# Feed-forward's first product by Strassen's seven half-sized ones, norms' roots on GpSimd, and a new instruction order

## The chip, the cores and the metric

One core of a Trainium2 chip runs the whole program. Its engines run side by side and wait for one another by semaphores: TensorE (PE, with weight loads shown apart as PEld), VectorE (DVE), ScalarE (ACT), GpSimd (POOL) and SyncE (SP), which issues nearly all DMAs. The metric is the device time of one execution in microseconds (us), the median of several runs.

## The reference

A transformer block on x of 2048 tokens by 512, all in float32: an attention part with 32 heads and a memory over four segments, then a feed-forward with a squared relu. Both have an adaptive norm before them.

```python
h = _layernorm(x) * (1 + ca) + sa
x = x + ga * _A_ref(h, A_wq, A_wk, A_wv, A_wo, A_beta)
h = _layernorm(x) * (1 + cb) + sb
x = x + gb * _B_ref(h, B_w1, B_b1, B_w2, B_b2)

def _B_ref(x, w1, b1, w2, b2):
    h = jnp.einsum("bsd,df->bsf", x, w1) + b1      # 512 -> 1792
    r = jnp.where(h > 0, h, 0)
    return jnp.einsum("bsf,fd->bsd", r * r, w2) + b2
```

## The kernel before

Each float32 operand is split into a rounded high part (fp32r) and the rest, its low part, and a product is three products: high by high, high by low, low by high.

Tokens are worked on in four sections s of 512. Attention runs section by section and makes up the first part of the program; its scores, masks and exponentials keep DVE and ACT busy beside PE. Each section's first norm, `ln1`, takes sums (`ln_stats`), one root for four token tiles at once (`ln_rstd`, L586-L595) and a scaling (`ln_apply`, L598), then transposes on PE. `ln_rstd` is eleven small DVE steps that need each other: epsilon, a first guess by integer arithmetic, three Newton steps. `ln2`, the second norm before the feed-forward, uses the same helpers.

After attention comes the output projection (`wo_tile`, sums bwop), which adds x and leaves the result in X1, one 512-column tile for each of 16 token tiles g, kept on chip. Then the feed-forward: W1 has 14 blocks f of 128 columns, loaded and split into high and low parts once (`load_w1`, tiles wr and W1) and kept; W2 as well (`load_w2`). For each section and block, `ffn1` makes 12 products of 512 columns into one bank (bh, L1357-L1359), ACT applies relu and square (r, rr; L1367, L1371), DVE squares again in full precision and takes the low part (L1374, L1375). `ffn2` multiplies rr with W2, for four token tiles, into four banks bpf (L1385-L1387) that sum over all f.

What stands in which order: every step is an `op` with an engine, a cost, a due time and its needs. A planner (`Plan`) holds buffers as pools with a number of slots (`POOLS`); a step that needs a slot (`get`) comes after the one that gives it back (`put`). The table `ORDER` lists each engine's steps by number and fixes the order; each engine works through its own list strictly. So a step that waits holds up all behind it on its engine. `z` and `e` are due times for the later stages. r had one slot, rr three, wr two.

## Time and profile before

| | us |
|---|---|
| median of 3 runs (785.7 to 787.88) | 787.33 |
| the profiled execution | 789.56 |
| its span, first to last instruction | 787.8 |
| mean granted TensorE clock | 0.992 of full |
| HBM read / written | 29.91 / 7.34 MB |

On the page, a line of a group has the source line, the engine, the operation, output<-inputs, shapes and count, then busy us and mean ns of one, then the idle time before them with what ended it. A busy time of PE counts modelled ends, so only start-to-start times tell its real pace. The chain of waits follows the last instruction back to what released it.

### The profile page before, as it was taken

The page shows a single profiled execution, that of the slowest core. Times are in us where ns is not written, and L with a number is a line of the kernel's source. Part 1 is how long each engine was busy: PE and PEld are TensorE (multiplying, and loading weights), DVE is VectorE, ACT ScalarE, POOL GpSimd, SP SyncE. Part 2 cuts the span into 40 slices and gives each one's busy share as a digit, 9 for nine tenths or more (in the row PEclk, how much of TensorE's full clock was granted, in tenths as well). Part 3 has the DMA queues.
Part 4 walks back from the last instruction along what each step waited for, and adds up shares of the span by engine and source line. Part 5 has one row for each costly group of instructions (what it writes and reads, how often), then busy time and mean ns, then how long its engine had stood idle before and what let it go on. Part 6 is the DMA issues. An engine that isn't in the chain of part 4 may idle for free. (4 is left out here: it accounts for less than half of the span.)

```text
span 787.8 us, 16571 instructions
## 1 busy us (share of the span) xinstructions
PE 770.6 (98%) x6072; PEld 579.4 (74%) x6075; DVE 533.5 (68%) x1493; ACT 429.0 (54%) x908; POOL 221.2 (28%) x334
## 2 busy tenths in 40 slices
...
GB/s 266 173 175 88 190 212 42 96 97 42 124 96 89 90 76 92 78 115 132 142 115 56 68 136 123 103 67 15 0 1 1 0 107 1 0 1 54 0 1 54
DMA packets 51306, 65.33 MB, mean 83 GB/s; under 512 B 7829, under 2 KB 24985, under 8 KB 51226
## 3 DMA queue, kind: packets, MB, share of 16 engines
...
q10 hardware_dynamic: 152, 0.13, 0.1%
HBM read 29.91 MB, written 7.34 MB: 47 GB/s over the span
## 5 line engine op out<-in xcount | busy, mean ns | idle before, releaser
L863 DVE CUSTOM_DVE_ANT_0 ba<-ba,msk 128x512 f32<-128x512 f32 (+2 forms) x384 | 185.7, 543 | 33.0 <-PE ba L858 29.2
L1045 ACT ACTIVATE pt<-bpb 128x512 f32<-128x512 f32 x320 | 170.7, 619 | 23.4 <-PE bpb L1028 22.0
L1374 DVE TENSOR_TENSOR r<-r 128x512 f32<-128x512 f32 x56 | 38.7, 691 | 139.0 <-ACT rr L1371 138.9
L745 PE MATMUL bqk<-HT,WQK 64*128 64x512 f32 x720 | 105.5, 402 | 2.7 <-DVE mx L863 2.6
L1032 POOL TENSOR_SCALAR_AFFINE_SELECT pt<-pt 128x512 f32<-128x512 f32 x128 | 80.3, 646 | 85.8 <-ACT pt L1045 47.0
L1367 ACT ACTIVATE r<-bh,b1c 128x512 f32<-128x512 f32 x56 | 38.5, 688 | 115.1 <-PE bh L1359 62.0
L1385 PE MATMUL bpf<-W,rr 128*128 128x512 f32 x224 | 87.9, 392 | 0.5 <-DVE X1L L1235 0.5
L1386 PE MATMUL bpf<-W,rr 128*128 128x512 f32 x224 | 87.7, 391 | 0.0
L1387 PE MATMUL bpf<-W,rr 128*128 128x512 f32 x224 | 87.6, 391 | 0.0
L1028 PE MATMUL bpb<-ST 64*128 64x256 f32 (+2 forms) x512 | 80.0, 354 | 2.1 <-DMA ST<-mt 0.8
L1087 PE MATMUL bpv<-pt,VT 128*32 128x512 f32 (+3 forms) x1024 | 80.9, 440 | 0.1
L745 PEld LDWEIGHTS bqk<-HT,WQK 64*128 64x128 f32 x720 | 70.8, 187 | 11.5 <-DVE mx L863 3.0
L858 PE MATMUL ba<-ST 63*128 63x256 f32 (+2 forms) x512 | 77.4, 347 | 1.0 <-DVE mx L863 0.4
L858 PEld LDWEIGHTS ba<-ST 63*128 63x128 f32 x512 | 50.9, 187 | 24.9 <-ACT pt L1045 4.3
L1371 ACT ACTIVATE rr<-r 128x512 fp32r<-128x512 f32 x56 | 35.4, 632 | 59.2 <-PE bpf L1387 58.4
L1028 PEld LDWEIGHTS bpb<-ST 64*128 64x128 f32 x512 | 51.3, 186 | 21.1 <-ACT pt L1045 4.4
L863 DVE DVE_READ_ACCUMULATOR2_ANT mx<- 128x1 f32 x384 | 54.2, 141 | 0.0
L825 PE MATMUL bv<-WVO,HT 64*128 64x512 f32 x384 | 53.3, 395 | 0.0
L1087 PEld LDWEIGHTS bpv<-pt,VT 128*32 128x32 f32 x1024 | 27.6, 109 | 33.2 <-issue 27.5
L1385 PEld LDWEIGHTS bpf<-W,rr 128*128 128x128 f32 x224 | 42.1, 188 | 10.2 <-DVE X1L L1235 0.9
L1386 PEld LDWEIGHTS bpf<-W,rr 128*128 128x128 f32 x224 | 42.1, 188 | 9.2
L1387 PEld LDWEIGHTS bpf<-W,rr 128*128 128x128 f32 x224 | 42.0, 188 | 9.2
...
## 6 DMA issues: line engine op xcount, KB each, us to landing
ST<-sg SPq DMA_DIRECT2D x192, 128.0 KB
...
```

What stands on the lines that cost most here:

```text
L745: m = nc.tensor.matmul(bank(("qk", u, w)), W3(w, k, x, cc * P, (cc + 1) * P)[z], HT[z, y, k], start=(ph == 0 and k == 0 and i == 0), stop= ...
L825: m = nc.tensor.matmul(bank(("v", s, t)), HT[z, x, k, t * P:(t + 1) * P], WVO[z, k, y], start=(ph == 0 and k == 0 and i == 0), stop=(ph == ...
L858: nc.tensor.matmul(dst[:, c0:c0 + n], ST[b:b + 63, 0, sl, qt * P:(qt + 1) * P], ST[b:b + 63, 1, sl, :n], start=True, stop=True)
L863: nc.vector.tensor_tensor_reduce(i, i, msk[:, 512 - n:], scale=1.0, scalar=-3e38, op0=ALU.add, op1=ALU.max, accum_out=o)
L1028: nc.tensor.matmul(dst, ST[b:b + 64, 1, sl, kb * P:(kb + 1) * P], ST[b:b + 64, 0, sl, q0:512], start=True, stop=True)
L1032: nc.gpsimd.affine_select(out=ap, in_=ap, pattern=[[0, ap.shape[1]], [1, P]], compare_op=ALU.is_ge, fill=0.0, base=0, channel_multiplier=-1)
L1045: ns = [act(512, lambda j=j: nc.scalar.activation(buf("PPP"[n], pt)[:, i + j], bank(keys[j]), AF.Exp, scale=0.25), pr[slot] + 0.01 + 0.001 ...
L1087: nc.tensor.matmul(bank(o)[32 * hq:32 * hq + 32, q0:q0 + src.shape[1]], v[:, a:a + 32], src, start=start, stop=stop, tile_position=(0, 32 ...
L1374: n = dve(580, lambda: nc.vector.tensor_tensor(TL[r], TL[r], TL[r], op=ALU.mult), pr + 0.01, after=[h], put=[r])
L1385: nc.tensor.matmul(p, rh, FF["W2"][:, f, 0], start=(f == 0), stop=False)
L1386: nc.tensor.matmul(p, rh, FF["W2"][:, f, 1], start=False, stop=False)
L1387: nc.tensor.matmul(p, rl, FF["W2"][:, f, 0], start=False, stop=(f == NF - 1))
```

## The change

It has three parts, which the planner's table ties together.

**Strassen.** A pair q of W1 blocks (256 columns) by 512 tokens, with the 512 inner rows in halves, is a product of 2x2 blocks. Instead of eight half-sized products (24 matmuls of 512 columns with the three-way split) there are seven of six matmuls of 256 columns each, on sums and differences of blocks. The sums of the tokens' side are made by `ln2` (four, `sub`; the array H2 now has seven blocks), those of W1 by `load_w1` (four, L1404). W1 is no longer kept: it is loaded, summed and split anew for every section (tiles w1r and w1d, two slots each). The products go into two banks, bhx and bhy, and are added on DVE into u and r (one slot each), over which relu, square and the copy to rr run on ACT for the whole pair. X1 of sections 0 to 2 no longer stays on chip: it is stored to HBM and loaded again for `ln2` and for the last sum (tiles x1, xh, xf, six slots together).

**Roots.** `ln_rstd` becomes two GpSimd steps, an addition and a power of -0.5.

**Order.** All five lists of `ORDER` are new, made with a cost under which VectorE and GpSimd do not run at once.

The core of the diff:

```diff
 ORDER = {
     "PE": """
-16 43 27 20 37 63 82 81 84 62 72 79 22 29 28 50 40 51 30 67 52 45 34 18 32 65 80 3 85 23 38 56 78 48 59 77 24 21 60 58
+16 67 26 82 79 74 73 31 37 75 53 27 40 28 78 35 39 50 63 81 17 29 76 54 33 68 65 85 51 83 24 45 3 58 47 77 61 25 32 19
...
+    mhalf = const.tile([P, 4], F32)
+    MHN = op("POOL", 0.1, lambda: nc.gpsimd.memset(mhalf, -0.5), -5.0)
     def ln_rstd(mvs, n):
-        v = small.tile([P, n], F32, name="lnv")
-        y = small.tile([P, n], F32, name="lny")
-        t = small.tile([P, n], F32, name="lnt")
         var = mvs[:, :, 1]
-        nc.vector.tensor_scalar(v, var, EPS_LN, None, op0=ALU.add)
-        nc.vector.tensor_scalar(y.bitcast(I32), v.bitcast(I32), -0.5, float(0x5F3759DF), op0=ALU.mult, op1=ALU.add)
-        for it in range(3):
-            nc.vector.scalar_tensor_tensor(t, y, -0.5, y, op0=ALU.mult, op1=ALU.mult)
-            nc.vector.tensor_tensor(t, t, v, op=ALU.mult)
-            nc.vector.scalar_tensor_tensor(var if it == 2 else y, t, 1.5, y, op0=ALU.add, op1=ALU.mult)
+        nc.gpsimd.tensor_scalar(var, var, EPS_LN, None, op0=ALU.add)
+        nc.gpsimd.tensor_tensor(var, var, mhalf[:, :n], op=ALU.pow)
...
-        r = op("DVE", 2.16, lambda: ln_rstd(TL[mv], 4), p_stat + 0.05, after=st)
+        r = op("POOL", 0.5, lambda: ln_rstd(TL[mv], 4), p_stat + 0.05, after=[*st, MHN])
...
+        keep = [] if last or s == 0 else [("x1", g)]
+        X1N[g] = op("DVE", 0.8, lambda: ln_stats(x1(g), st_all[:, g]), pr + 0.06, after=[n], put=keep)
+        if not last:
+            X1D[g] = sp(lambda: nc.sync.dma_start(x1_dram[s][(g % 4) * P:(g % 4 + 1) * P, :], x1(g)), pr + 0.055, 1 << 18, lat=1.3,
+                        after=[n], put=keep)
...
+        def split(n, i, j, b):
+            v = lambda: tl(i, j).rearrange("p (k n) -> p k n", k=2)
+            h = act(512, lambda: nc.scalar.copy(h2(s, b)[:, 0], v()), pr[2] + 0.02, sbuf=True, after=[*n, *wait])
+            lo = op("DVE", 0.6, lambda: nc.vector.tensor_tensor(h2(s, b)[:, 1], v(), h2(s, b)[:, 0].bitcast(F32), op=ALU.subtract),
+                    pr[2] + 0.03, after=[h], put=[kk(i, j)] if b > 2 else ())
+            H2N[s][b] = [h, lo]
+            return [lo]
+        def sub(o, a, b, after):
+            return op("DVE", 0.6, lambda: nc.vector.tensor_tensor(tl(*o), tl(*a), tl(*b), op=ALU.subtract), pr[2] + 0.025, after=after,
+                      put=[kk(*a), kk(*b)])
...
+            if i == 0:
+                l00 = split(F[0][0], 0, 0, 0)
+                l10 = split(F[0][1], 0, 1, 1)
+        l11 = split(F[1][1], 1, 1, 2)
+        t1 = sub((0, 0), (1, 0), (0, 0), l00 + F[1][0])
+        t3 = sub((1, 0), (1, 1), (1, 0), [t1] + F[1][1])
+        t2 = sub((1, 1), (1, 1), (0, 0), [t1, t3] + l11)
+        t4 = sub((0, 1), (0, 1), (1, 1), [t2] + l10)
+        split([t1], 0, 0, 3)
+        split([t2], 1, 1, 4)
+        split([t3], 1, 0, 5)
+        split([t4], 0, 1, 6)
...
-    def load_w1(f, pr):
-        k = ("wr1", f)
-        wv_ = lambda: wraw(k).rearrange("p (k n) -> p k n", k=KD)
-        n = sp(lambda: nc.sync.dma_start(wv_(), w1[:, f * P:(f + 1) * P].rearrange("(k p) n -> p k n", p=P)), pr - 0.2,
-               1 << 18, after=[N_FFN], get=[("wr", k)])
-        n = act(512, lambda: nc.scalar.copy(FF["W1"][:, f, 0], wv_()), pr, sbuf=True, after=[n], put=[k])
-        W1N[f] = dve(512, lambda: nc.vector.tensor_tensor(FF["W1"][:, f, 1], wv_(), FF["W1"][:, f, 0].bitcast(F32), op=ALU.subtract),
-                     pr + 0.01, after=[n], put=[k])
+    def load_w1(s, q, pr):
+        kr, kd = ("w1r", s, q), ("w1d", s, q)
+        def load():
+            TL[kr] = FF["sb"].tile([P, 4, 2, P], F32, name="w1r", tag=f"w1r{PL.slot[kr]}")
+            for h in (0, 1):
+                f = 2 * q + h
+                nc.sync.dma_start(TL[kr][:, 2 * h:2 * h + 2].rearrange("p a k n -> p (a k) n"),
+                                  w1[:, f * P:(f + 1) * P].rearrange("(k p) n -> p k n", p=P))
+        def hi(a, b, o):
+            if kd not in TL:
+                TL[kd] = FF["sb"].tile([P, 2, 7, 2, P], F32R, name="w1d", tag=f"w1d{PL.slot[kd]}")
+            nc.scalar.copy(TL[kd][:, 0, o:o + b - a], TL[kr][:, a:b])
+        def lo(a, b, o):
+            nc.vector.tensor_tensor(TL[kd][:, 1, o:o + b - a], TL[kr][:, a:b], TL[kd][:, 0, o:o + b - a].bitcast(F32), op=ALU.subtract)
+        def sums():
+            r = TL[kr]
+            for o, a, b, f in ((1, 0, 1, ALU.add), (0, 2, 0, ALU.subtract), (2, 1, 2, ALU.subtract), (3, 3, 2, ALU.subtract)):
+                nc.vector.tensor_tensor(r[:, o], r[:, a], r[:, b], op=f)
+        n = sp(load, pr - 0.2, 1 << 19, 2, after=[N_FFN], get=[("w1r", kr)])
+        h = act(768, lambda: hi(1, 4, 0), pr, sbuf=True, after=[n], get=[("w1d", kd)])
+        l = dve(768, lambda: lo(1, 4, 0), pr + 0.01, after=[h])
+        n = op("DVE", 1.36, sums, pr + 0.02, after=[l])
+        h2_ = act(1024, lambda: hi(0, 4, 3), pr + 0.03, sbuf=True, after=[n])
+        l2_ = dve(1024, lambda: lo(0, 4, 3), pr + 0.04, after=[h2_], put=[kr])
+        W1N[s, q] = ([h, l], [h2_, l2_])
...
-    def ffn1(s, f, pr):
-        i = s * NF + f
-        b, r, rr = ("h", s, f), ("r", s, f), ("rr", s, f)
-        def mm(k):
-            h2 = LT["H2"][s % 2]
-            p = bank(b)
-            wh, wl = FF["W1"][:, f, 0, k], FF["W1"][:, f, 1, k]
-            nc.tensor.matmul(p, wh, h2[:, 0, k], start=(k == 0), stop=False)
-            nc.tensor.matmul(p, wh, h2[:, 1, k], start=False, stop=False)
-            nc.tensor.matmul(p, wl, h2[:, 0, k], start=False, stop=(k == KD - 1))
-        n = None
-        for k in range(KD):
-            n = pe("F", 0.699, lambda k=k: mm(k), pr + 0.001 * k, after=[n] if k else [W1N[f], *H2N[s]], get=() if k else [("#D", b)])
-        F1[s, f] = n
-        def relu():
-            TL[r] = FF["sb"].tile([P, 512], F32, name="r", tag=f"r{PL.slot[r]}")
-            nc.scalar.activation(TL[r], bank(b), AF.Relu, bias=b1c[:, f:f + 1])
-        def square():
-            TL[rr] = FF["sb"].tile([P, 2, 512], F32R, name="rr", tag=f"rr{PL.slot[rr]}")
-            nc.scalar.activation(TL[rr][:, 0], TL[r], AF.Square)
-        n = act(512, relu, pr + 0.01, sc=1, after=[n, n_b1], get=[("r", r)], put=[b])
-        h = act(512, square, pr + 0.011, sbuf=True, after=[n], get=[("rr", rr)])
-        n = dve(580, lambda: nc.vector.tensor_tensor(TL[r], TL[r], TL[r], op=ALU.mult), pr + 0.01, after=[h], put=[r])
-        n = dve(512, lambda: nc.vector.tensor_tensor(TL[rr][:, 1], TL[r], TL[rr][:, 0].bitcast(F32), op=ALU.subtract), pr + 0.012,
-                after=[n, h], put=[r])
-        return n
+    def ffn1(s, q, pr):
+        x, y, kd = ("hx", s, q), ("hy", s, q), ("w1d", s, q)
+        r, rr, u = ("r", s, q), ("rr", s, q), ("u", s, q)
+        wa, wb = W1N[s, q]
+        B = H2N[s]
+        def mm(a, b, key, c):
+            w, m, p = TL[kd], h2(s, b), bank(key)[:, 256 * c:256 * c + 256]
+            for k in (0, 1):
+                nc.tensor.matmul(p, w[:, 0, a, k], m[:, 0, k], start=k == 0, stop=False)
+                nc.tensor.matmul(p, w[:, 0, a, k], m[:, 1, k], start=False, stop=False)
+                nc.tensor.matmul(p, w[:, 1, a, k], m[:, 0, k], start=False, stop=k == 1)
+        def prod(i, key, c, pr, after, **kw):
+            a, b = {1: (1, 0), 2: (2, 1), 3: (6, 2), 4: (0, 6), 5: (4, 3), 6: (5, 4), 7: (3, 5)}[i]
+            return pe("F", 0.712, lambda: mm(a, b, key, c), pr + 0.001 * i, after=[*(wa if a < 3 else wb), *B[b], *after], **kw)
+        rt = lambda: TL[r]
+        two = lambda t: t.rearrange("p (c n) -> p c n", c=2)
+        def u1():
+            TL[u] = FF["sb"].tile([P, 2, 256], F32, name="u", tag=f"u{PL.slot[u]}")
+            nc.scalar.copy(TL[u][:, 0], bank(x)[:, :256])
+        def u34():
+            TL[r] = FF["sb"].tile([P, 4, 256], F32, name="r", tag=f"r{PL.slot[r]}")
+            nc.vector.tensor_tensor(rt()[:, 0:4:3], two(bank(y)), TL[u][:, 1:2, :].to_broadcast([P, 2, 256]), op=ALU.add)
+        def add(o, a, b):
+            return lambda: nc.vector.tensor_tensor(o(), a(), b(), op=ALU.add)
+        p1 = prod(1, x, 0, pr, [], get=[("#D", x)])
+        n1 = act(256, u1, pr + 0.001, after=[p1], get=[("u", u)])
+        p6 = prod(6, x, 1, pr + 0.01, [p1])
+        n2 = dve(256, add(lambda: TL[u][:, 1], lambda: TL[u][:, 0], lambda: bank(x)[:, 256:]), pr + 0.011, after=[p6, n1])
+        p7 = prod(7, y, 0, pr + 0.02, [p6], get=[("#D", y)])
+        p5 = prod(5, y, 1, pr + 0.03, [p7])
+        n3 = dve(512, u34, pr + 0.031, after=[p5, n2], get=[("r", r)])
+        n4 = dve(256, add(lambda: rt()[:, 1], lambda: rt()[:, 0], lambda: bank(y)[:, 256:]), pr + 0.032, after=[n3])
+        p2 = prod(2, x, 0, pr + 0.04, [p5, n1, n2])
+        n5 = dve(256, add(lambda: rt()[:, 2], lambda: TL[u][:, 0], lambda: bank(x)[:, :256]), pr + 0.041, after=[p2, n3], put=[x, u])
+        p4 = prod(4, y, 0, pr + 0.05, [p2, n4])
+        p3 = prod(3, y, 1, pr + 0.06, [p4], put=[kd])
+        F1[s, q] = p3
+        n6 = dve(512, add(lambda: rt()[:, 0:4:3], lambda: rt()[:, 0:4:3], lambda: two(bank(y))), pr + 0.061, after=[p3, n4], put=[y])
+        def relu(i):
+            nc.scalar.activation(rt()[:, 2 * i:2 * i + 2], rt()[:, 2 * i:2 * i + 2], AF.Relu, bias=b1c[:, 2 * q + i:2 * q + i + 1])
+        a = [act(512, lambda i=i: relu(i), pr + 0.062 + 0.001 * i, sbuf=True, sc=1, after=[n6, n4, n5, n_b1]) for i in (0, 1)]
+        def high():
+            TL[rr] = FF["sb"].tile([P, 2, 4, 256], F32R, name="rr", tag=f"rr{PL.slot[rr]}")
+            nc.scalar.copy(TL[rr][:, 0], rt())
+        n = act(1024, lambda: nc.scalar.activation(rt(), rt(), AF.Square), pr + 0.064, sbuf=True, after=a)
+        h = act(1024, high, pr + 0.065, sbuf=True, after=[n], get=[("rr", rr)])
+        n = dve(1024, lambda: nc.vector.tensor_tensor(TL[rr][:, 1], rt(), TL[rr][:, 0].bitcast(F32), op=ALU.subtract), pr + 0.066,
+                after=[h], put=[r])
+        return [h, n]
...
+        if f == NF - 3:
+            n = X1L2[g]
+            if s < NS - 1:
+                n = sp(lambda: nc.sync.dma_start(xt_(), x1_dram[s][t * P:(t + 1) * P, :]), pr - 0.5, 1 << 18, after=[X1D[g], N_FFN], get=[("x1", xf)])
+            F2[s, t, "x"] = dve(512, lambda: nc.vector.tensor_tensor(xt_(), xt_(), gab, op=ALU.add), pr, after=[n_b2, n])
...
-        for f in range(NF):
-            RR[s, f] = ffn1(s, f, z + ST2 * (s * NF + f))
+            ln2(s, [z + ST2 * ((s - 1) * NF + 4 + 2 * t) for t in range(4)], [F1[s - 2, q] for q in range(NF // 2)] if s > 1 else WOL)
+        for q in range(NF // 2):
+            if s:
+                load_w1(s, q, z + ST2 * (s * NF + 2 * q - 3))
+            RR[s, q] = ffn1(s, q, z + ST2 * (s * NF + 2 * q))
```

Three places in the order. First, the root of section 2's first norm, in attention. On DVE before, sg is a query or key tile, lnv, lny and lnt are the root's small tiles, mv the norm's sums:

```order
L784 TENSOR_TENSOR sg<-bqk,sg 128x512
L590 TENSOR_SCALAR lnv<-mv 128x4
L591 TENSOR_SCALAR lny<-lnv 128x4
L593 SCALAR_TENSOR_TENSOR lnt<-lny 128x4
L594 TENSOR_TENSOR lnt<-lnt,lnv 128x4
L595 SCALAR_TENSOR_TENSOR lny<-lnt,lny 128x4
```

Six more steps like the last three follow. Now it stands on GpSimd, between attention's masks (pt) and a marker of one element (hinge):

```order
L806 TENSOR_TENSOR phi0_1870<-phi0_1870,e_1873 128x512
L1044 AFFINE_SELECT pt_1791<-pt_1791 128x4x128
L603 TENSOR_SCALAR mv_1689<-mv_1689 128x4
L604 TENSOR_TENSOR mv_1689<-mv_1689,mhalf_117 128x4
L516 MEMSET hinge_s_116 1x1
```

Eleven steps left DVE, and two joined GpSimd's queue behind its larger ones.

Second, DVE where the feed-forward begins. Before, oT is the output projection's low part, wr a raw block and W1 its split:

```order
L1228 TENSOR_TENSOR oT_7704<-bwot_7690,oT_7704 128x512
L1326 TENSOR_TENSOR W1_7678<-wr_7686,W1_7678 128x512
L1326 TENSOR_TENSOR W1_7678<-wr_7688,W1_7678 128x512
L1326 TENSOR_TENSOR W1_7678<-wr_7728,W1_7678 128x512
L1228 TENSOR_TENSOR oT_7756<-bwot_7747,oT_7756 128x512
L1326 TENSOR_TENSOR W1_7678<-wr_7735,W1_7678 128x512
```

Now, with the first pair's raw w1r_7653 and split w1d_7690:

```order
L1399 TENSOR_TENSOR w1d_7690<-w1r_7653,w1d_7690 128x768
L1404 TENSOR_TENSOR w1r_7653<-w1r_7653 128x256 x4
L1416 TENSOR_TENSOR wr_7669<-wr_7669,gbb_7652 128x512
L1416 TENSOR_TENSOR wr_7671<-wr_7671,gbb_7652 128x512
L1257 TENSOR_TENSOR X1L_70<-bwop_7686,xw_7676 128x512
L1399 TENSOR_TENSOR w1d_7690<-w1r_7653,w1d_7690 128x1024
```

The split of one pair is now three kinds of step, the last of which stands behind W2's scaling and a sum of the projection; the second pair's begins before the first pair's sums u and r.

Third, DVE in the middle of the feed-forward, section 2. Before:

```order
L1374 TENSOR_TENSOR r_9001<-r_9001 128x512
L621 TENSOR_SCALAR xh_8611<-blnq_8963,modc_78 128x256
L1395 TENSOR_TENSOR X11_6245<-bpf_8599,X11_6245 128x512
L1375 TENSOR_TENSOR rr_9005<-r_9001,rr_9005 128x512
L1374 TENSOR_TENSOR r_9050<-r_9050 128x512
```

Now:

```order
L1399 TENSOR_TENSOR w1d_9807<-w1r_9682,w1d_9807 128x768
L1404 TENSOR_TENSOR w1r_9682<-w1r_9682 128x256 x4
L1463 TENSOR_TENSOR u_9822<-u_9822,bhx_9757 128x256
L1489 TENSOR_TENSOR rr_9847<-r_9765,rr_9847 128x1024
L1460 TENSOR_TENSOR r_9864<-bhy_9825,u_9822 128x2x256
L1463 TENSOR_TENSOR r_9864<-r_9864,bhy_9825 128x256
L1510 TENSOR_TENSOR X1L_70<-X1L_70,gab_82 128x512
L1463 TENSOR_TENSOR r_9864<-u_9822,bhx_9757 128x256
```

Where two steps for each block stood, DVE now has W1's split for a later pair (L1399, L1404), the pair's own sums (L1463, L1460) and the low part of the pair before (L1489), which must be done before the next sum may write the single r.

More of the change, by code (lines that the diff above doesn't have):

```diff
@@ L393, in block_kernel @@
     dram = ctx.enter_context(tc.tile_pool(name="dram", bufs=1, space=bass.MemoryType.DRAM))
+    x1_dram = [dram.tile([L, D], F32, name=f"x1_dram{s}") for s in range(NS - 1)]
     o_dram = dram.tile([S, D], F32, name="o_dram")
```

372 lines of the change are left out of this document (204 added, 168 removed), and 12 rows, old and new, of the table ORDER.

## The prediction

> **What bounds the kernel now.** I read the page's busy times and chain of waits first, then the windows, then single rows.
>
> ```profile
> PE 770.6 (98%) x6072; PEld 579.4 (74%) x6075; DVE 533.5 (68%) x1493; ACT 429.0 (54%) x908; POOL 221.2 (28%) x334
> PE 36%; DMA 3%; DVE 2%; issue 1%; ACT 1%; POOL 0%; SPq 0%; POOLq 0%; DVEq 0%; ACTq 0%
> PE bpf L1386 6%; PE bpf L1387 6%; PE bpf L1385 6%; PE bh L1357 6%; PE bh L1358 6%; PE bh L1359 6%; DMA wr<-in_B_w 3%; PE blnq L607 1%; ACT pt L1045 0%; DVE W L1334 0%; DVE W L1326 0%; DVE wr L1332 0%; DVE r L1374 0%; POOL pt L1032 0%; DVE rr L1375 0%
> ```
>
> The chain's six named lines are all the feed-forward: there TensorE (PE) sets the end. The windows (columns: stretch, its length, then busy us and count of PE, PEld, DVE, ACT, POOL, granted clock, DMA share, GB/s) show two regimes.
>
> ```profile
> 150.00:200.00 50.00, 48.91 (x619) 33.96 (x617) 45.36 (x157) 41.95 (x98) 32.52 (x49) 1.00 0.30 72
> 400.00:440.00 40.00, 39.97 (x340) 27.49 (x336) 38.00 (x113) 25.15 (x53) 8.55 (x16) 1.00 0.24 73
> 459.00:540.00 81.00, 79.41 (x354) 64.09 (x354) 62.84 (x132) 34.62 (x60) 0.00 (x0) 1.00 0.35 101
> 540.00:620.00 80.00, 80.00 (x355) 65.00 (x355) 31.48 (x50) 22.04 (x36) 0.00 (x0) 1.00 0.00 1
> ```
>
> Attention (to about 455 us) has VectorE (DVE) at 45 of 50 us and 38 of 40. From 459 us PE is full and DVE is far from it. Whether "full" is true of modelled ends is settled by start-to-start times:
>
> ```profile
> 560.10 0.39 PE L1357 MATMUL bh<-WVO,W 128*128 128x512 f32 x1
> ...
> 574.98 0.40 PE L1386 MATMUL bpf<-W,rr 128*128 128x512 f32 x1
> 29.02 0.28 PE L737 MATMUL bqk<-HT,WQK 128*128 128x256 f32 x1
> ...
> 32.24 0.28 PE L737 MATMUL bqk<-HT,WQK 128*128 128x256 f32 x1
> 544.41 0.60 PE L607 MATMUL blnq<-ident,xh 128*128 128x128 f32 x4
> 544.76 0.48 PE L1357 MATMUL bh<-WVO,W 128*128 128x512 f32 x1
> ```
>
> Between the first two stand 64 steps: 14.88/64 = 0.2325 us for a 512-column product. Between the next two, 27 steps: 3.22/27 = 0.1193 us for a 256-column one of the same type with its own weight load. A transpose takes 0.35/4 = 0.0875. From the first bh (459.29) to the end of the last bpf (783.97) are 324.7 us; 1344 products of the feed-forward and 33 of the output projection at 0.2325, and 52 transposes, make 324.7. PE has no idle time there at all, so a product less is time less, as long as its suppliers keep up.
>
> **The change part by part.**
>
> *Products.* For two blocks of W1 (a pair) before issues 24 products of 512 columns, 24 x 0.2325 = 5.58 us; after issues 7 x 6 = 42 of 256, 42 x 0.1193 = 5.01. There are 4 x 7 = 28 pairs: 28 x 0.57 = **15.9 us less**. The second product stays at 5.58 a pair, so a pair now has 10.6 us of PE.
>
> A rule that speaks against it: the Trainium skill, Perfetto Trace Analysis, Identifying the Most-Contended Engine, says headroom on TensorE is to be judged by the weight loads' busy share, not by matmul busy time. The rows to weigh it by:
>
> ```profile
> 26.90 0.19 PEld L736 LDWEIGHTS bqk<-HT,WQK 128*128 128x128 f32 x1
> 27.02 0.19 PEld L737 LDWEIGHTS bqk<-HT,WQK 128*128 128x128 f32 x1
> ```
>
> Loads of 0.19 start every 0.12, so they overlap each other, and the 256-column products kept their 0.119. By the rule 66 loads a pair at 0.19 would take 12.5 us, more than the 10.6 that the products need; the rows speak for the 10.6.
>
> *VectorE in the feed-forward.* Its price by start-to-start times:
>
> ```profile
> 502.17 0.69 DVE L1375 TENSOR_TENSOR rr<-r,rr 128x512 fp32r<-128x512 f32 x1
> 502.77 0.69 DVE L1326 TENSOR_TENSOR W<-wr,W 128x512 fp32r<-128x512 f32 x1
> 439.45 0.42 DVE L965 TENSOR_TENSOR am<-bmr,den 128x256 f32<-128x256 f32 x1
> 439.79 0.25 DVE L1149 RECIPROCAL dn<-bfin 128x16 f32<-128x16 f32 x1
> 471.86 0.68 DVE L1374 TENSOR_TENSOR r<-r 128x512 f32<-128x512 f32 x1
> 472.58 0.69 DVE L1375 TENSOR_TENSOR rr<-r,rr 128x512 fp32r<-128x512 f32 x1
> ```
>
> 512 columns hold DVE for 0.60, 256 for 0.34, and a step that needs the one just before it starts 0.72 after it, 0.12 late. So 768 columns come to 0.87 and 1024 to 1.14, estimated on the same slope; a dependent 256 is 0.46. Per pair, evacuation was 4 x 0.60 = 2.4; it becomes 3 x 0.34 + 2 x 0.60 + 1.14 + 2 x 0.12 = 3.6. W1's split was 1.2 and done once; it becomes 0.87 + 4 x 0.46 + 1.14 = 3.85 in every section. In section 0 that is 7 x (1.2 + 2.65) = 27 us more, later 7 x 5.05 = 35. Each second norm takes seven more 512 steps (four sums, three splits: 4.2) and loses its root (2.2, below): 2 more. By the windows above, 459:540 would hold 62.8 + 29 = 92 us of DVE against 81 - 4 = 77 of PE: 15 too much. 540:620 would hold 31.5 + 37 = 68 against 76. Some of the surplus moves later, so I counted both engines along the changed order at these prices, from the first split on DVE and the first product on PE: DVE is about 10 us ahead in work from the third pair to the seventeenth (101 against 90 at the ninth, 152 against 141 at the fourteenth), and PE overtakes it only at the twenty-fifth. DVE may begin up to 5 us before PE's first product, so packed without a gap it holds PE back by 5; each of its waits for ACT, PE or a load in those 150 us adds to that. Bounds 0 (the surplus deferred to where PE has more) and 15; I take **+11**, nearer to the upper, since an engine that waits on three others is not packed without gaps. ACT rises to about 5.6 us a pair (a copy of 256, two relus, two passes of 1024, W1's 1.7) and stays hidden behind PE's 10.6; without that cover it would join the chain below.
>
> *A longer chain on one buffer.* r has one slot. Before, a block's chain was relu, square, product, low part; each fits between PE's other work:
>
> ```profile
> L1367 ACT ACTIVATE r<-bh,b1c 128x512 f32<-128x512 f32 x56 | 38.5, 688 | 115.1 <-PE bh L1359 62.0 <-DVE rr L1375 52.9
> L1371 ACT ACTIVATE rr<-r 128x512 fp32r<-128x512 f32 x56 | 35.4, 632 | 59.2 <-PE bpf L1387 58.4
> 442.56 4.05 ACT L1045 ACTIVATE pt<-bpb 128x512 f32<-128x512 f32 x8
> ```
>
> (Eight at 4.05: 0.51 apart.) After, from the fourth product of a pair to that of the next: two products 1.6, sum 0.69, two relus 1.3, square and copy of 1024 columns 1.1 each, low part 1.2, the next pair's first two sums 0.69 + 0.42: about 8.1 us. Behind the waiting sum on DVE's queue stand the next W1 splits, and PE's own queue is in order, so its later products wait too. The chain fits into 10.6, but the changed order puts only 7.7 to 11.2 us of PE work (median 9.2) between the third product of a pair and the fourth of the next; that part of the chain is 6.5 without anything queued in front, and one 1024-column step in front of a link costs 1.1. Bounds 0 and 0.5 x 28 = 14; where DVE sets the pace its stalls are counted already, so I take **+3**, nearer to the chain that fits.
>
> *Roots on GpSimd.* One root on DVE is eleven dependent steps:
>
> ```profile
> 473.19 0.17 DVE L590 TENSOR_SCALAR lnv<-st_all 128x4 f32<-128x4 f32 x1
> ...
> 475.17 0.17 DVE L595 SCALAR_TENSOR_TENSOR st_all<-lnt,lny 128x4 f32<-128x4 f32 x1
> L593 DVE SCALAR_TENSOR_TENSOR lnt<-lny 128x4 f32<-128x4 f32 x24 | 7.0, 294 | 0.8
> 193.99 1.22 POOL L1032 TENSOR_SCALAR_AFFINE_SELECT pt<-pt 128x512 f32<-128x512 f32 x2 [0.29 <-ACT pt L1045]
> 194.01 0.64 DVE L1151 TENSOR_TENSOR dn<-dn,omg 128x16 f32<-128x16 f32 x1
> 195.18 1.28 POOL L629 TENSOR_TENSOR HT<-xt,HT 128x512 fp32r<-128x512 f32 x1
> 195.31 1.19 DVE L1151 TENSOR_TENSOR dn<-dn,omg 128x16 f32<-128x16 f32 x1
> L1006 POOL TENSOR_TENSOR MB<-MB,tm 32x34 f32<-32x34 f32 x32 | 7.8, 245 | 1.4
> L793 POOL TENSOR_SCALAR e<-e 128x512 f32<-128x512 f32 x24 | 35.7, 1486 | 9.7 <-ACT e L789 9.6
> ```
>
> Alone it takes 2.15 us (473.19 to 475.34). The two L1151 rows, of 16 columns, end where GpSimd's instruction ends: VectorE steps with two SBUF inputs wait for GpSimd. That is why L593 means 294 ns, not 160. Five roots lie in attention (four first norms, section 0's second): 5 x 2.15 = 10.8 us of DVE, and the blocked time with it, perhaps 3. The power is in no row: two steps of four columns cost between 2 x 0.25 and 2 x 1.49 us; even 3.0 replaces 2.15 in the norm's own delay, and the norm stands well ahead of its use. POOL is 28% busy, so its queue has room; ahead of a root may stand 1.5 us. Nothing here excludes a loss.
>
> *The order.* Avoiding the blocked pairs can return up to the excess of L1151, L598 and the roots, some 10 us of DVE. Attention's DVE relief is thus 11 to 24 us at 85 to 95% use, and only part of it ends on PE. Bounds -18 and +4 (a new order that fits worse); I take **-7**.
>
> *Transition.* Section 0's seven extra 512 steps (4.2) fall into 400:440, where DVE has 38 of 40, and x1 now goes through 12 stores, on SP's queue past the W1 loads, and 20 loads. **+2** (0 to 5). W1 is read four times: 42 more loads of 256 KB. They lie beside an idle DMA (share 0.00 in 540:620); if that cover fails, a load that lands late stops a pair, for some microseconds each.
>
> **Sum**: -15.9 + 11 + 3 - 7 + 2 = -6.9. The profiled execution took 789.56 us (span 787.8), so 782.7; the median of the three runs is 2.2 lower: **780.5**. A measurement of this kernel can tell about 0.3% (2.4 us) from no change.
>
> **The rivals.**
> 1. *The surplus is deferred*: DVE's extra work finds room behind PE after all, and its relief in attention pays 10. -15.9 + 3 + 3 - 10 + 2 = -18: 769.5. For it: only 31 of 80 us of DVE are busy in 540:620. Against: 92 us of it in 77.
> 2. *Attention gains nothing*: PE, not DVE, ends the waits there, or the new order only shifts them. -15.9 + 11 + 3 + 0 + 2 = 0: 787.5, no change. For it: PE is 49 of 50 busy in 150:200, though by modelled ends.
> 3. *Slower: the pair's chain sets the pace.* Without its term the sum is -9.9, so from 0.35 us of stall a pair (28 x 0.35) the change loses. With a 1024-column step in front at one link in most pairs, 0.8 us: 28 x 0.8 = 22, -9.9 + 22 = +12: 799.5. For it: one slot of r, two queues in order. Against: median 9.2 us of PE work in the place of 6.5.
> 4. *The products do not shrink*: weight loads bind at 0.19, 12.5 us a pair against 11.2 before: 28 x 1.3 = +36, with -7 + 2 near 818. The 0.119 rows speak against it. It is the time that the rule of Perfetto Trace Analysis in the Trainium skill would suggest.
>
> **How the numbers follow.** Forecast (774 to 787): 0.44. Rival 1 (758 to 774): 0.22. Rival 2 (785 to 790): 0.13. Rival 3 (790 to 808): 0.18. Rival 4: 0.03. Faster (below 785): 0.22 and most of the forecast's 0.44: 0.60; within 0.3%: the rest of it and two thirds of rival 2: 0.13; slower: 0.27. The range 762 to 801 leaves out about 0.15 of these. Both signs hold much of the chance, so the forecast's own range, 774 to 787, stands beside it.
>
> **What would show it.** bhx and bhy products at 0.12 start to start confirm the first term. In the windows from 455 us: PE gaps ended by DVE w1d or r in the first 90 us are the second term (VectorE), PE gaps ended by DVE r in all four sections the chain's. The attention terms together (-7 + 2) need the first product against a block of W1 at about 454 us, and 459.29 or later would refute it. The forecast is wrong if the feed-forward's stage (324.7 before) is not 315 to 330 us long, or if its start moves by over 15.

## The result, and the profile after

| | before | after |
|---|---|---|
| first timing, 4 runs each | 786.83 us (785.7 to 787.88) | 778.83 us (774.6 to 781.16) |
| ratio, 95% interval | | 0.9893 [0.9847, 0.9938] |
| second timing, 11 and 5 runs | 787.35 us | 776.87 us |
| ratio, 95% interval | | 0.9857 [0.9836, 0.9879] |
| profiled execution, span | 789.56, 787.8 us | 778.38, 776.7 us |
| first product against W1 | 459.29 us | 460.46 us |
| from it to the last bpf's end (the stage) | 324.7 us | 312.6 us |

The kernel is 8 to 10.5 us faster; 780.5 was predicted. The profiled execution is 11.2 us shorter: the feed-forward's stage 12.1 less, its start 1.2 later. So the total came near while its parts did not: the stage was to be 315 to 330 us long and took 312.6, and its start was to be near 454 us.

The page after (busy times, then the chain of waits):

```profile
PE 756.3 (97%) x6576; PEld 594.2 (77%) x6579; DVE 643.3 (83%) x1643; ACT 509.2 (66%) x990; POOL 233.6 (30%) x351
PE 69%; DVE 16%; ACT 6%; issue 3%; SPq 3%; DMA 2%; POOL 1%; ACTq 0%; DVEq 0%; POOLq 0%
```

VectorE went from 68 to 83% busy. Its 16% of the chain can't be set against the 2% of before: that chain reaches back only to 440 us, this one to the program's start. Between the first product against W1 and the last bpf's end, VectorE is 78.6 of the 312.6 us of this chain. The same windows as before (busy us of PE, PEld, DVE, ACT, POOL, then granted clock, DMA share, GB/s):

```profile
150.00:200.00 50.00, 49.45 (x613) 33.25 (x609) 42.74 (x154) 42.02 (x97) 32.34 (x48) 0.97 0.23 61
400.00:440.00 40.00, 39.68 (x322) 26.40 (x321) 35.34 (x91) 27.59 (x59) 11.15 (x18) 1.00 0.41 123
459.00:540.00 81.00, 79.96 (x503) 70.45 (x502) 79.05 (x137) 51.00 (x74) 0.00 (x0) 1.00 0.39 114
540.00:620.00 80.00, 79.54 (x502) 70.90 (x501) 75.33 (x130) 49.02 (x67) 0.00 (x0) 1.00 0.34 103
```

Attention lost 2.6 us of VectorE in each of the first two stretches. In 459:540 PE and DVE both read as full. By this view alone neither can be called the bound; the runs below had to tell. Single rows of the changed kernel (start, length, engine, line) give the product's price and the stage's start:

```profile
460.46 0.37 PE L1443 MATMUL bhx<-H2a,w1d 128*128 128x256 f32 x1
460.67 0.28 PE L1444 MATMUL bhx<-H2a,w1d 128*128 128x256 f32 x1
460.79 0.28 PE L1445 MATMUL bhx<-H2a,w1d 128*128 128x256 f32 x1
460.90 0.28 PE L1443 MATMUL bhx<-H2a,w1d 128*128 128x256 f32 x1
461.02 0.28 PE L1444 MATMUL bhx<-H2a,w1d 128*128 128x256 f32 x1
461.13 0.28 PE L1445 MATMUL bhx<-H2a,w1d 128*128 128x256 f32 x1
```

From the second to the sixth are 0.46/4 = 0.115 us each: 0.12, as forecast, with a weight load for each. (Over the whole stage of w1_one_sum below, the 1176 products take 140.9 us from start to next start, 0.120 each.) PEld is busy 70.9 of 80 us and binds nothing: in the run w1_one_sum below, where TensorE never waits in the feed-forward, it is busier still (windows, columns as above):

```profile
460.00:540.00 80.00, 79.98 (x514) 72.22 (x513) 71.87 (x118) 53.11 (x77) 0.00 (x0) 1.00 0.42 126
```

### The profile page after: what moved, and what is told of

It reads as the page before. It is cut to its first block, busy times and chain, and to the rows that moved or that the text cites. A ratio compares the mean times of both kernels' runs of the same rounds, so it can differ in the third digit from the quotient of the medians.

```text
span 776.7 us, 17899 instructions
## 1 busy us (share of the span) xinstructions
PE 756.3 (97%) x6576; PEld 594.2 (77%) x6579; DVE 643.3 (83%) x1643; ACT 509.2 (66%) x990; POOL 233.6 (30%) x351
## 4 chain that ended last, share of the span: by engine, by line
PE 69%; DVE 16%; ACT 6%; issue 3%; SPq 3%; DMA 2%; POOL 1%; ACTq 0%; DVEq 0%; POOLq 0%
PE bqk L757 9%; PE bpv L1099 6%; PE bpf L1502 5%; PE bpf L1504 5%; PE bpf L1503 5%; PE ba L870 5%; PE bpb L1040 5%; PE bv L837 4%; PE bhy L1443 3%; PE bhy L1444 2%; PE bhy L1445 2%; ACT pt L1057 2%; SPq L812 2%; PE bwarm L546 2%; DVE w1r L1404 2%
## 5 line engine op out<-in xcount | busy, mean ns | idle before, releaser
L875 DVE CUSTOM_DVE_ANT_0 ba<-ba,msk 128x128 f32<-128x128 f32 (+2 forms) x384 | 186.0, 542 | 33.9 <-PE ba L870 27.1
L1057 ACT ACTIVATE pt<-bpb 128x512 f32<-128x512 f32 x320 | 173.3, 616 | 31.2 <-PE bpb L1040 27.6
L1396 ACT CAST w1d<-w1r 128x768 fp32r<-128x768 f32 (+1 forms) x56 | 52.7, 944 | 76.5 <-PE bhy L1445 58.2
L757 PE MATMUL bqk<-HT,WQK 64*128 64x512 f32 x720 | 101.6, 396 | 0.0
L870 PE MATMUL ba<-ST 63*128 63x256 f32 (+2 forms) x512 | 75.1, 346 | 1.0 <-issue 0.4
L870 PEld LDWEIGHTS ba<-ST 63*128 63x128 f32 x512 | 48.8, 187 | 19.4 <-issue 4.2
L1399 DVE TENSOR_TENSOR w1d<-w1r,w1d 128x768 fp32r<-128x768 f32 (+1 forms) x56 | 60.6, 1085 | 3.2 <-ACT w1d L1396 2.8
L1404 DVE TENSOR_TENSOR w1r<-w1r 128x256 f32<-128x256 f32 x112 | 47.5, 424 | 3.2
L1481 ACT ACTIVATE r<-r,b1c 128x512 f32<-128x512 f32 x56 | 38.4, 719 | 17.8 <-DVE r L1463 17.5
L1504 PEld LDWEIGHTS bpf<-W,rr 128*128 128x128 f32 x224 | 42.0, 188 | 10.0 <-DVE rr L1489 0.3
```

The lines of the kernel that those rows point to most:

```text
L757: m = nc.tensor.matmul(bank(("qk", u, w)), W3(w, k, x, cc * P, (cc + 1) * P)[z], HT[z, y, k], start=(ph == 0 and k == 0 and i == 0), stop= ...
L870: nc.tensor.matmul(dst[:, c0:c0 + n], ST[b:b + 63, 0, sl, qt * P:(qt + 1) * P], ST[b:b + 63, 1, sl, :n], start=True, stop=True)
L875: nc.vector.tensor_tensor_reduce(i, i, msk[:, 512 - n:], scale=1.0, scalar=-3e38, op0=ALU.add, op1=ALU.max, accum_out=o)
L1057: ns = [act(512, lambda j=j: nc.scalar.activation(buf("PPP"[n], pt)[:, i + j], bank(keys[j]), AF.Exp, scale=0.25), pr[slot] + 0.01 + 0.001 ...
L1404: nc.vector.tensor_tensor(r[:, o], r[:, a], r[:, b], op=f)
L1504: nc.tensor.matmul(p, rl, FF["W2"][:, f, 0], start=False, stop=(f == NF - 1))
```

## The experiments

All were timed against the kernel before on the same chip. "After" in the comparisons is the second timing, 0.9857. At 787.5 us, 0.001 of ratio is 0.8 us.

**Attention: the order and the roots.** Two kernels exchange attention between before and after, as far as the instruction lists can be joined; a third moves the roots alone. A fourth has the old order, but all roots on GpSimd, with the new feed-forward.

attn_old_ffn_new: the lists of ORDER up to about 390 us in before's sequence, and

```diff
-        r = op("POOL", 0.5, lambda: ln_rstd(TL[mv], 4), p_stat + 0.05, after=[*st, MHN])
+        r = op("DVE", 2.16, lambda: ln_newton(TL[mv], 4), p_stat + 0.05, after=st)
```

> The changed kernel with the old order of the attention's instructions on every engine up to about 390 us of the plan, and with the first norms' roots back on VectorE; from there on, and in the whole feed-forward, it is the changed kernel. Theory N (the new order and the roots on GpSimd bought nothing that reached the feed-forward): as the changed kernel, 776 to 781 us, ratio to the kernel before 0.986 to 0.992, first product against W1 at 459 to 462 us. Theory P (the prediction's: they bought 5 to 7 us, lost again where attention hands over to the feed-forward): 783 to 787 us, first product against W1 5 us later than in the changed kernel (460.46).

Measured: 780.88 us, 0.9896 [0.9875, 0.9917].

attn_new_ffn_old: the kernel before with after's lists up to about 410 us and, for the first norms,

```diff
-        r = op("DVE", 2.16, lambda: ln_rstd(TL[mv], 4), p_stat + 0.05, after=st)
+        r = op("POOL", 0.5, lambda: ln_power(TL[mv], 4), p_stat + 0.05, after=[*st, MHN])
```

> The kernel before with the changed kernel's order of the attention's instructions up to about 410 us of the plan and the first norms' roots on GpSimd; the end of attention, the hand-over and the feed-forward are those of before. Theory N: 786 to 790 us (the place where the two orders are joined may cost 0 to 4 us), first product against W1 at 458 to 463 us. Theory P: 780 to 783 us, that product at 453 to 455 us.

Measured: 786.73 us, 0.9980 [0.9961, 0.9999].

roots_only: the same line, before's lists.

> The kernel before, old order everywhere, only the four first norms' roots moved from VectorE to GpSimd. Theory N: 786 to 789 us (8.6 us of VectorE less, none of it ends on TensorE). Theory P: half or more of the 8.6 us arrives, 781 to 784 us. A third: the power of 1.05 us and the step of 0.23 to 0.45 us before it stand in front of other GpSimd work and the old order does not fit them: 788 to 792 us.

Measured: 784.51 us, 0.9956 [0.9936, 0.9976].

old_order_roots_ffn_new: attn_old_ffn_new without its diff line, the roots at their old places in the order.

> The changed kernel with the old order of attention up to about 390 us of the plan and all roots on GpSimd. The roots alone, in the kernel before, were worth 3.5 us (ratio 0.9956); the new order with the roots 1.6 us (0.998). Theory R (the roots pay, the new order gives half of it back): 1.5 to 3 us faster than the changed kernel, 3 to 4 us faster than the same with the roots on VectorE (0.9896), ratio 0.985 to 0.987. Rival (what attention gains is lost again at the hand-over, where the new feed-forward waits for something else): as the changed kernel within 1 us.

Measured: 777.01 us, 0.9858 [0.9835, 0.9881].

The roots alone are worth 3.5 us in the old kernel (interval 1.9 to 5.0); theory N falls there, and theory P's half of 8.6 us, 4.3, is inside the interval. In the new one they are worth about 3 (0.9896 to 0.9858; these two intervals overlap by a little). The new order adds nothing in the new kernel (0.9858 to 0.9857, each known to about 2 us); joined to the old feed-forward it stands 1.9 us behind the roots alone, but these intervals overlap too, and the joint may cost that. Theory R's second half falls: the new kernel is no faster with the old order, so the new order gave nothing back there, and it gained nothing that can be measured. The root's price on GpSimd, grouped by form (busy us, mean ns):

```profile
L604 POOL TENSOR_TENSOR mv<-mv,mhalf 128x4 f32<-128x4 f32 x4 | 4.2, 1046 | 0.3
L603 POOL TENSOR_SCALAR mv<-mv 128x4 f32<-128x4 f32 x4 | 0.9, 228 | 3.0 <-DVE mv L596 2.9
```

1.27 us together, inside the bounds of 0.5 and 3.0.

**VectorE in the feed-forward.** First the changed kernel once more, beside the next runs:

> The changed kernel itself, timed beside the next three on one chip: ratio to the kernel before 0.985 to 0.992, 777 to 781 us at this chip's level of the kernel before.

Measured: 776.87 us, 0.9857 [0.9836, 0.9879]; stage 312.6.

w1_one_sum takes VectorE work away; three of four sums are left out, so the products are of other numbers:

```diff
-            for o, a, b, f in ((1, 0, 1, ALU.add), (0, 2, 0, ALU.subtract), (2, 1, 2, ALU.subtract), (3, 3, 2, ALU.subtract)):
+            for o, a, b, f in ((1, 0, 1, ALU.add),):
```

> The changed kernel with one of the four sums on W1's quarters for each pair; the other three are left out, so VectorE has 3 x 0.46 = 1.4 us less in each of 28 pairs and TensorE the same work. Theory D (VectorE, packed without a gap, sets the pace for the first ten or so pairs, and holds TensorE back by 5.7 us in all): 4 to 5.5 us faster than the changed kernel, 773 to 775 us, ratio 0.981 to 0.985, the gain all there by the eleventh pair. Rival E (TensorE sets the pace, VectorE's work is hidden): 777 to 780 us. The prediction's size (11 us from VectorE): 767 to 769 us.

Measured: 771.17 us, 0.9778 [0.9754, 0.9802]: 6.2 us under after, more than theory D's 4 to 5.5 and less than the prediction's 11. The stage itself is 308.2 us, 4.4 less, as D has it, and TensorE alone is 307.0 us of its chain of waits. Of the other 1.8 us the two profiles show 0.4 ahead of the stage (458.96 against 459.39); what is left is inside the intervals.

w1_low_twice adds VectorE work:

```diff
-        l = dve(768, lambda: lo(1, 4, 0), pr + 0.01, after=[h])
+        l = dve(768, lambda: (lo(1, 4, 0), lo(1, 4, 0)), pr + 0.01, after=[h])
```

> The changed kernel with the first low part of W1 (768 columns, 0.95 us) computed twice for each pair: 28 x 0.9 = 25 us more on VectorE, nothing else. Theory D (VectorE paces the first half of the feed-forward, TensorE overtakes it late): by the count of both engines' work VectorE is then ahead until the twenty-fourth pair, by up to 18.6 us instead of 5.7, so 11 to 14 us more than the changed kernel, with the feed-forward's stage at 324 to 327 us (312.6). Rival E (TensorE paces): 0 to 4 us more.

Measured: 793.59 us, 1.0078 [1.0060, 1.0097]; stage 330.3. That is 17.4 us more for 28 x 0.96 = 27 us of work: theory D's direction, but more than its 11 to 14, and the stage is over its 324 to 327. The second pass also stands in front of the links of r's chain, and TensorE waits 6.8 us for r there (1.1 in after_again); that this is the surplus was not tested.

Where the time goes shows in VectorE's L1460, the sum that each pair makes once after its fourth product (p5). The first product against W1, then the ninth and the twenty-eighth L1460, of after_again:

```profile
459.39 0.37 PE L1443 MATMUL bhx<-H2a,w1d 128*128 128x256 f32 x1
554.67 0.69 DVE L1460 TENSOR_TENSOR r<-bhy,u 128x512 f32<-128x512 f32 x1
756.42 0.69 DVE L1460 TENSOR_TENSOR r<-bhy,u 128x512 f32<-128x512 f32 x1
```

and of w1_one_sum:

```profile
458.96 0.37 PE L1443 MATMUL bhx<-H2a,w1d 128*128 128x256 f32 x1
550.26 0.69 DVE L1460 TENSOR_TENSOR r<-bhy,u 128x512 f32<-128x512 f32 x1
751.58 0.69 DVE L1460 TENSOR_TENSOR r<-bhy,u 128x512 f32<-128x512 f32 x1
```

After its first product, after_again needs 95.28 us to the ninth pair and w1_one_sum 91.30: 4.0 behind. At the last pair it is 297.03 against 292.62: 4.4. The same difference, pair by pair, for the runs with this feed-forward on which this part and the next ones rest (us behind w1_one_sum, each worked out from such rows and counted from its own first product):

| pair | 1 | 3 | 5 | 7 | 9 | 10 | 13 | 17 | 21 | 28 |
|---|---|---|---|---|---|---|---|---|---|---|
| after_again | 0.3 | 0.9 | 2.2 | 3.1 | 4.0 | 3.8 | 3.8 | 4.6 | 5.3 | 4.4 |
| trans_full | 0.4 | 1.0 | 2.3 | 3.2 | 4.0 | 3.9 | 3.9 | 4.7 | 5.3 | 4.4 |
| trans_order | 4.5 | 5.0 | 6.3 | 7.3 | 8.1 | 8.0 | 8.0 | 8.8 | 9.5 | 8.6 |
| half_square | 0.3 | 0.9 | 2.2 | 3.1 | 4.0 | 3.8 | 3.4 | 4.1 | 4.8 | 3.7 |
| gate_late_trans | 0.3 | 0.3 | -0.1 | -0.2 | 0.1 | 2.9 | 2.9 | 6.6 | 7.3 | 7.6 |
| w1_low_twice | 1.1 | 3.6 | 6.5 | 9.5 | 12.3 | 13.1 | 15.0 | 19.4 | 21.9 | 22.1 |
| chain_longer | 0.4 | 2.3 | 4.4 | 6.5 | 8.6 | 9.5 | 11.5 | 15.8 | 19.6 | 23.4 |

The changed kernel's loss is made in pairs 1 to 9 and stays. The prediction's count had 101 us of VectorE's work to the ninth L1460. In the first profile after, the rows of VectorE's first split of W1 and of that sum are:

```profile
456.26 0.96 DVE L1399 TENSOR_TENSOR w1d<-w1r,w1d 128x768 fp32r<-128x768 f32 x1 [0.52 <-ACT w1d L1396]
555.71 0.69 DVE L1460 TENSOR_TENSOR r<-bhy,u 128x512 f32<-128x512 f32 x1
```

From the start of the one to the end of the other are 100.1 us, and VectorE is idle in only 2.4 of them, in pieces of at most 0.33: it is packed. In w1_one_sum the same stretch is 95.5 us long, with 9.5 idle.

**The chain on r.** chain_longer doubles one step of it on ScalarE, and leaves VectorE's work alone:

```diff
             nc.scalar.copy(TL[rr][:, 0], rt())
+            nc.scalar.copy(TL[rr][:, 0], rt())
```

> The changed kernel with the copy of r to its high part (1024 columns, about 1.05 us on ScalarE) done twice for each pair: r's chain is 1.05 us longer in each of 28 pairs, VectorE and TensorE have the same work. Theory S (the chain has room: with three sums left out the stage came to 308.2 us, which is TensorE's work alone, so the chain's term is nothing): 0 to 2 us more than the changed kernel. Rival C (the chain is at its limit where VectorE isn't): from 10 us up to 28 x 1.05 = 29 us more, with TensorE's gaps ended by r in all four sections.

Measured: 795.42 us, 1.0094 [1.0068, 1.0119]; stage 331.2, so 18.6 us more for 28 x 1.05 = 29. Theory S falls. In its windows (columns as above) TensorE loses 2 to 3.6 us each, in 580:620 too, where it is busy for all 40.00 us in the changed kernel:

```profile
460.00:540.00 80.00, 76.45 (x475) 66.42 (x474) 74.90 (x130) 54.11 (x76) 0.00 (x0) 1.00 0.36 112
540.00:580.00 40.00, 37.93 (x233) 32.97 (x233) 36.25 (x62) 27.01 (x36) 0.00 (x0) 1.00 0.44 139
580.00:620.00 40.00, 37.61 (x238) 32.83 (x237) 34.55 (x60) 24.39 (x35) 0.00 (x0) 1.00 0.16 47
```

and among its waits (waited for: us in total, times, longest) r's are by far TensorE's largest:

```profile
PE bhy L1443 <- DVE r L1463: 11.1, 19, 1.6
```

half_square shortens the chain; the squaring of half of r is left out:

```diff
-        n = act(1024, lambda: nc.scalar.activation(rt(), rt(), AF.Square), pr + 0.064, sbuf=True, after=a)
+        n = act(1024, lambda: nc.scalar.activation(rt()[:, 0:2], rt()[:, 0:2], AF.Square), pr + 0.064, sbuf=True, after=a)
```

> The changed kernel with the squaring of half of r left out (512 columns squared in the place of 1024), so r's chain is 0.4 us shorter in each of 28 pairs and VectorE's work is the same. Chain longer by 1.05 us cost 18.6 us of the feed-forward's stage. Theory D (as the changed kernel stands, VectorE alone holds TensorE back, in pairs 1 to 9, by 4 us; the chain just fits): stage 311.5 to 313 us (312.6), the loss against w1_one_sum in pairs 1 to 9 as before, 0 to 1 us faster. Rival C (the chain with VectorE's queue in it is what costs): a good part of the 4 us comes back, stage 308.5 to 310.5 us, 2 to 4 us faster.

Measured: 777.45 us, 0.9856 [0.9832, 0.9879]; stage 312.1. Pairs 1 to 9 lose the same to a tenth: theory D. So the chain costs the changed kernel next to nothing (0.5 us of stage), but by an estimate from chain_longer it has room for only (1.05 x 28 - 18.6)/28 = 0.4 us a pair.

**The hand-over from attention.** The changed kernel's rows of TensorE around 450 us:

```profile
448.79 0.40 PE L1216 MATMUL bwop<-WVO,oT 128*128 128x512 f32 x1
449.12 0.46 PE L1134 MATMUL bfin<-ident,oraw 64*128 64x64 f32 x8
449.85 0.46 PE L1134 MATMUL bfin<-ident,oraw 64*128 64x64 f32 x8 [0.27 <-POOL hinge_s L516]
450.25 0.55 PE L1241 MATMUL bwot<-ident,X1L 128*128 128x128 f32 x3
453.40 0.78 PE L1241 MATMUL bwot<-ident,X1L 128*128 128x128 f32 x5 [2.60 <-DVE X1L L1170]
454.48 0.80 PE L1214 MATMUL bwop<-WVO,oT 128*128 128x512 f32 x1 [0.30 <-ACT oT L1248]
455.07 0.63 PE L1215 MATMUL bwop<-WVO,oT 128*128 128x512 f32 x1
455.50 0.63 PE L1216 MATMUL bwop<-WVO,oT 128*128 128x512 f32 x1
455.92 0.63 PE L1214 MATMUL bwop<-WVO,oT 128*128 128x512 f32 x1
...
457.54 0.40 PE L1215 MATMUL bwop<-WVO,oT 128*128 128x512 f32 x1
```

and its windows there, with the granted clock third from the end:

```profile
450.00:455.00 5.00, 2.10 (x17) 1.51 (x16) 3.65 (x11) 1.07 (x2) 3.01 (x4) 0.90 0.67 187
455.00:460.00 5.00, 5.00 (x18) 3.92 (x17) 4.34 (x9) 1.74 (x2) 0.00 (x0) 0.76 0.93 276
```

The last attention block waits 2.60 us for VectorE. From 454.48 to 457.54 seven products of 512 columns take 3.06 us instead of 7 x 0.2325 = 1.63, where the window's granted clock is 0.76: 1.4 more. Together 4.0 us. Before, nine products of section 2's output projection stood behind the last transposes of attention (bfin) and filled that wait; in the changed order all of that projection stands ahead of these transposes.

trans_order puts three of section 2's groups of products back behind the last product of probabilities and values (bpv) on TensorE, two of them behind the last bfin as well, and section 2's last addition and norm statistics (L1257, L595) behind the last L1170 on VectorE. trans_full also moves the store of that sum on SP (operation 2628) behind the first loads of W1 and W2:

```diff
-    N_FFN = op("NIL", 0.0, open_ffn, -20.0, after=list(PL.nodes))
+    N_FFN = op("NIL", 0.0, open_ffn, -20.0, after=[n for n in PL.nodes if n not in (X1N[11], X1D[11])])
- 2562 2574 2606 2424 2618 2617 2584 2573 2628 2667 2665 2677 2673 2795 2681 2666 3285 2695 2691 2687 2765 2775 2785
+ 2562 2574 2606 2424 2618 2617 2584 2573 2667 2665 2677 2673 2628 2795 2681 2666 3285 2695 2691 2687 2765 2775 2785
```

> The changed kernel with another order at the hand-over: three of the last four groups of section 2's output projection stand behind the last transposed attention block on TensorE, its addition and norm statistics behind the last attention norms on VectorE, its store behind the first loads of W1 and W2 on SP. TensorE's 2.6 us gap ahead of the last section's transposes should shrink to under 1.5 us. Theory D (from the first split of W1 on VectorE sets the pace, so only an earlier first split counts, 456.26 us in the changed kernel): 0 to 2 us faster than the changed kernel, by as much as that split is earlier. Rival G (the gap and the lowered clock after it cost the 4 us that separate 460.46 from the forecast's 454): 3 to 4 us faster.

Measured: 773.31 us, 0.9818 [0.9803, 0.9834], 3.1 us under the changed kernel and the fastest of all. Its first split of W1 is at 451.80 us (454.31 in after_again), its first product at 455.50, its stage 312.60. Its rows of TensorE at the same place:

```profile
447.82 0.40 PE L1216 MATMUL bwop<-WVO,oT 128*128 128x512 f32 x1
448.06 0.49 PE L1241 MATMUL bwot<-ident,X1L 128*128 128x128 f32 x3
449.22 0.77 PE L1241 MATMUL bwot<-ident,X1L 128*128 128x128 f32 x5 [0.68 <-DVE X1L L1170]
450.31 0.50 PE L1214 MATMUL bwop<-WVO,oT 128*128 128x512 f32 x1 [0.31 <-ACT oT L1248]
450.64 0.39 PE L1215 MATMUL bwop<-WVO,oT 128*128 128x512 f32 x1
```

and the second of the two windows:

```profile
455.00:460.00 5.00, 5.00 (x35) 4.46 (x34) 5.00 (x9) 3.47 (x7) 0.00 (x0) 1.00 0.58 132
```

The gap is 0.68 us, and the clock stays at 1.00. The 3.1 us lie in rival G's range and over theory D's 0 to 2; by D's own rule, though, a split that is 2.5 us earlier allows about as much. trans_order tells them apart:

> The changed kernel with only TensorE's and VectorE's order at the hand-over changed as in trans_full; SP's order is the old one, so the first loads of W1 still stand behind the store of section 2's last tile, whose addition now comes later. Theory D (what counts is when VectorE can split the first W1 block): that split no earlier than in the changed kernel (454.3 us in its second profile), and 0 to 3 us slower than it. Rival G (TensorE's gap and the clock after it): 2 to 3 us faster than it, as trans_full.

Measured: 780.11 us, 0.9897 [0.9873, 0.9921], 3.2 us over the changed kernel, though its gap is 0.65 us and its clock 1.00 up to 460 us. Its first split of W1, and TensorE's longest wait behind it, are the rows

```profile
457.36 0.96 DVE L1399 TENSOR_TENSOR w1d<-w1r,w1d 128x768 fp32r<-128x768 f32 x1 [4.14 <-ACT w1d L1396]
463.21 0.39 PE L1445 MATMUL bhx<-H2a,w1d 128*128 128x256 f32 x1 [1.41 <-DVE w1d L1399]
```

The split comes at 457.36, after 4.14 us of idle time. TensorE starts on W1 at 457.38, earlier than in the changed kernel, waits for the splits, and its stage then takes 316.8 us; by the table the loss is there at the first pair. The times follow the split: 3.05 us later and 3.2 slower here, 2.5 earlier and 3.1 faster in trans_full. So a smaller gap is worth nothing when the split comes later; rival G falls.

The store's move without the rest was not run. In the changed kernel it could have brought little, by these rows of ScalarE:

```profile
453.84 1.07 ACT L1248 CAST oT<-bwot 128x512 fp32r<-128x512 f32 x2 [5.59 <-PE bwot L1241]
455.40 0.83 ACT L1396 CAST w1d<-w1r 128x768 fp32r<-128x768 f32 x1 [0.49 <-DMA w1r<-in_B_w]
```

The first copy of W1 stands behind a step that needs TensorE's late transposes, and waits only another 0.49 us for its load. So with an earlier load alone the split would be about 0.5 us earlier, by estimate: both parts of trans_full seem to be needed.

**A relief that keeps the result.** gate_late_trans is trans_full with W2's gate taken off the first section:

```diff
-        n = dve(512, lambda: nc.vector.tensor_tensor(wraw(k), wraw(k), FF["gbb"], op=ALU.mult), pr, after=[n, n_gbb])
+        n = dve(512, lambda: None, pr, after=[n, n_gbb])
...
+                    nc.vector.tensor_tensor(bank(b)[:, c_], bank(b)[:, c_], FF["gbb"][:, c_], op=ALU.mult)
                     nc.vector.tensor_tensor(xt_()[:, c_], bank(b)[:, c_], xt_()[:, c_], op=ALU.add)
```

> trans_full with W2's columns not multiplied by the gate while W2 is split (14 steps of 512 columns on VectorE less in the first 120 us of the feed-forward, 8.4 us); the products' sum is multiplied by the gate instead, before the last addition (16 or so steps of 0.6 us more, spread over the four sections). Theory D: VectorE no longer holds TensorE back, the feed-forward's stage goes from 312.6 to 308.5 to 310 us, 769 to 771 us in all, ratio 0.977 to 0.979. Rival E (VectorE's share is not what costs): stage 312 to 314 us, 773 to 775 us.

Measured: 778.70 us, 0.9875 [0.9853, 0.9897], 4.5 us over trans_full by the ratios; stage 315.8. A miss on the total, but the table says why: pairs 1 to 9 lose nothing any more, as D has it. Then 2.8 us go between pairs 9 and 10, and more from 15 to 17 and at 24: just behind each section's end, where eight steps on VectorE now close a section in the place of four. TensorE's waits in its feed-forward are

```profile
PE bhy L1443 <- DVE r L1463: 2.8, 5, 0.9
PE bhx L1443 <- DVE u L1463: 0.9, 2, 0.7
PE bpf L1502 <- DVE xf L1517: 0.9, 2, 0.5
```

4.6 us, against 1.5 in trans_full, whose stage is 3.2 us shorter. L1517 is itself one of the closing steps: TensorE waits for its bank. That the closing steps also make r and u late, by standing in front of their sums, fits, but was not tested.

## Why the prediction was right, and where it was not

| term | predicted | measured | by |
|---|---|---|---|
| products | -15.9 | -16.5 | stage of before, 324.7, to that of w1_one_sum, 308.2 |
| VectorE in the feed-forward | +11 | +4.4 | 308.2 to 312.6 |
| chain on r | +3 | about 0 | half_square: 0.5 of stage |
| roots and order | -7 | -3 to -3.5, all roots | roots_only, old_order_roots_ffn_new |
| transition | +2 | about +4 | what is left of the 11.2; 2.60 + 1.4 by its rows |

*Products*: right. With VectorE relieved, the stage is TensorE's work alone, 16.5 us less. Of these, 0.7 are three products of the output projection that stood behind the first product against W1 before (33 of them) and stand ahead of it now (30 left); without them it is 15.8.

*VectorE*: the mechanism and the count were right. The wrong step was the choice between the bounds: "nearer to the upper, since an engine that waits on three others is not packed without gaps". It was packed, to 2.4 of 100.1 us, and the number that the prediction gave for that case, 5 us, was nearly the price. The sign that was named, PE gaps ended by w1d or r in the first 90 us, barely showed. The largest of TensorE's waits in the feed-forward (after_again) is

```profile
PE bhy L1443 <- DVE r L1463: 1.1, 4, 0.4
```

while 4.0 us are lost. The pace of the pairs shows them.

*Chain*: the choice of the end near nothing was right, its reason only half. The room was taken as 10.6 against 8.1 (its two products are 12 x 0.1193 = 1.4 us there, not 1.6); by the runs it is about 0.4. So the third rival, slower from 0.35 us of stall a pair, did not come true, but a chain some tenths longer would have begun to cost.

*Attention*: the test was a first product at about 454 us, "459.29 or later would refute". It came at 460.46, and at 459.39 in the second profile: refuted. What VectorE gave up for the new order did not end on TensorE; the second rival's mechanism is right for the order, and wrong for the roots, which paid about 3 us of their 8.6 on VectorE.

*Transition*: the +2 was for stores, loads and VectorE's steps. What was lost was another thing, the products that used to cover the last norms, and the clock after them; the 0.7 us of products that moved ahead of the stage are in it as well. The prediction allowed for a new order that fits worse only in a bound (+4). And TensorE's rows are not the whole of it: by trans_order the loss comes back only together with an earlier first split on VectorE.

*Products that do not shrink* (the fourth rival): out, by the 0.115 us and the 308.2 us.

The total came out by cancelling: 7 and 3 us too much for VectorE and the chain, 4 too much gain in attention, 2 too little loss behind it. That it came within 2 to 4 us is therefore luck; by the prediction's own sign, a stage of 315 to 330 us, the forecast is wrong, and by its other one, a start near 454, so are its terms for attention. A slip in its chances changed nothing: the rest of the forecast's chance (0.06) and two thirds of rival 2 make 0.15 within 0.3%, not 0.13.
